# A transformer kernel with a built-in planner: layernorm without its product column, epsilon on GpSimd, DMA transposes planned at new prices

## The chip, the cores and the metric

The kernel runs on one core of one Trainium2 chip. The core has a matrix engine (TensorE, PE in the profile; its weight loads are listed as PEld), three engines for elementwise work (VectorE or DVE, ScalarE or ACT, GpSimd or POOL), and a queue that issues transfers (SyncE, SP). SBUF is the on-chip memory, PSUM the accumulators that TensorE writes, in eight banks of 128 x 512 float32. The metric is device time of one execution in microseconds (us); the median of several runs counts, and less is better.

## The reference

Two layers of a transformer block on 2048 tokens of width 512 in bfloat16, with 32 heads of 16 columns and a hidden width of 1792. Layernorm has no gain and no offset. Both layers use the same weights.

```python
def _layernorm(x, axis=-1, eps=1e-5):
    m = jnp.mean(x, axis=axis, keepdims=True)
    v = jnp.var(x, axis=axis, keepdims=True)
    return (x - m) / jnp.sqrt(v + eps)

def _A_ref(x, wqkv, wo):           # H = 32, Dh = 16
    q, k, v = ...(x @ wqkv)...
    scores = jnp.einsum("bhqd,bhkd->bhqk", q, k) * (Dh ** -0.5)
    o = jnp.einsum("bhqk,bhkd->bhqd", _softmax(scores, axis=-1), v)
    return ...o... @ wo

def _B_ref(x, w1, b1, w2, b2):
    h = _gelu(jnp.einsum("bsd,df->bsf", x, w1) + b1)
    return jnp.einsum("bsf,fd->bsd", h, w2) + b2

x = A_x
x = x + _A_ref(_layernorm(x), A_wqkv, A_wo)
x = x + _B_ref(_layernorm(x), B_w1, B_b1, B_w2, B_b2)
x = x + _A_ref(_layernorm(x), A_wqkv, A_wo)
x = x + _B_ref(_layernorm(x), B_w1, B_b1, B_w2, B_b2)
```

## The kernel before

**Tiles and stages.** The 2048 tokens are 16 tiles of 128 (the partitions) and four chunks of 512. Attention works on cells: a cell is one head, one tile of keys and 512 queries (for the last chunk two heads and 256), 4096 cells in all. A score matmul (L1244) writes a cell into one PSUM bank. Most cells are then exponentiated by ScalarE (L1601), two or three cells to an instruction, into a ring of buffers (`pt`, with parts of `kt`, `q` and `v` lent to it when they are free). The other cells go to VectorE and GpSimd, which approximate the exponential with 16-bit integers: L1396 evicts the cell from PSUM on VectorE, L1473 adds a shift, mostly on GpSimd, and L1478 adds a second shift on VectorE; the buffers are `du`. Only the key tiles listed in `KD` may go that way. A value matmul (L1665) sums either kind of cell into one bank; for a cell of VectorE it takes four of them, three with scaled copies of the values (`vc`). Beside attention, the work of the previous chunk runs: the output projection, the feed-forward part (`hpair`, L976, `gelu`, L997, `ytile`), and the next layer's projections.

**Layernorm** (`ln` and `ln_tile`) comes in groups of one, two or four tiles. For each tile VectorE takes statistics (L666) and aggregates them to a mean and a variance in `mv` (L668). For the group, VectorE adds epsilon (L671, `varr`), GpSimd raises the result to the power -0.5 (L673, `rstd`), and VectorE forms the product -mean x rstd (L676, `nmr`). For each tile one instruction then gives x * rstd + nmr in bfloat16 (L689, `xln`): on GpSimd as a rule, on VectorE where `quick` is set, which holds for the first four tiles of the kernel and the last two. After the GpSimd form a DMA transpose is issued on SP (L693) and lands in `kt`, `xf` or `xp`; after the VectorE form TensorE transposes (L700). The ring `xln` has two buffers, so the third tile's L689 needs the first transpose to have landed.

**The order** of every engine's instructions is fixed when the kernel is built, by a planner written in the kernel (`_Sched`). Threads in Python yield operations (`_Op`) with an engine, a cost, the keys they read and write, and a `tail`, the time from the end of its cost to the landing of a transfer. The planner keeps a clock for each engine, computes when an operation's inputs are ready, and at each step starts the operation that can start first, by priority. `LATENCY` is added between an operation's end and those that wait for it, `OVERLAP` is taken off each VectorE cost, `OWN` and `HEAD` adjust waits on VectorE and on the port that it shares with GpSimd in the planner's model (`port`). `TOL` decides in `attach` whether a free bank may take a VectorE cell, `PSHIFT` in `dchain` whether L1473 goes to GpSimd or to VectorE, `SLACK` and `LATE` how long a score matmul may wait. `fill` puts matmuls without use (L1232, into banks that are free) ahead of a gap of TensorE while the planned activity of the last `WINDOW` microseconds lies below `WARM`. The chosen order is then emitted with semaphore waits; on the chip each engine's queue is strictly in that order, whatever the durations turn out to be. SP's queue holds the loads of weights into an eight-part ring (L933), those of x, the transposes and the stores of the output, also in the planned order.

Of the kernel before, what the change touches and what calls it, by code (L numbers as in the profile page):

```python
# [5 lines left out]
ALU = mybir.AluOpType  # L6
ACT = mybir.ActivationFunctionType
BF16 = mybir.dt.bfloat16
F32 = mybir.dt.float32
# [19 lines left out]
XT = 8  # L29
# [19 lines left out]
OPENING = 18  # L49
ROUNDS = 2  # L50
PTLOW = 5
TOL = 0.2
EVAC = 0.4
MID = 1.4
ENDS = 0.9
QUEUE = 4
RUSH = 4
WINDOW = 3.4
WARM = 2.3
FMARGIN = -0.1  # L60
FOLD = 0.1
COLD = 8
# [8 lines left out]
DWIDE = 2  # L71
RWIDE = 2
AHEAD = 24
PSHIFT = 3
LOG2E = 1.4426950408889634
E_SCALE = 0.25 * LOG2E * 128
E_BIAS = 15992.765054484162
# [6 lines left out]
class _Prog:  # L84
# [4 lines left out]
    def __init__(self, sems):  # L89
        self.sems = sems  # L90
        self.cnt = {k: 0 for k in sems}
        self.prog = {e: [] for e in self.ENGS}
        self.K = {e: {} for e in self.ENGS}
        self.ev_k = {}
        self.lastw = {}
        self.reads = {}
# [89 lines left out]
class _Op:  # L186
    __slots__ = ("eng", "cost", "fns", "reads", "writes", "sem", "by", "tail", "prio", "mode", "slack", "late", "back", "port", "limit", "after")

    def __init__(self, eng, cost, fns, reads=(), writes=(), sem=None, by=1, tail=0.0, prio=None, mode="F", slack=None):
        self.eng, self.cost = eng, cost  # L190
        self.fns = fns if isinstance(fns, list) else [fns]
        self.reads, self.writes = list(reads), list(writes)
        self.sem, self.by, self.tail, self.prio, self.mode, self.slack = sem, by, tail, prio, mode, slack
        self.limit = 1e9
        self.late, self.after = None, []
        self.port = eng == "dve" and self.writes[:1] != [] and self.writes[0].startswith(("OTT", "NMR"))


class _Thread:
# [7 lines left out]
        self.done = False  # L207


OWN = 0.022  # L210
HEAD = 0.14
LATENCY = {"pe": 0.2175, "act": 0.21, "dve": 0.139, "pool": 0.153328, "sp": 0.1}
OVERLAP = 0.083
ROUND = 1.02


class _Sched:
# [76 lines left out]
    def _ready(self, op):  # L294
# [4 lines left out]
        for ev in self.P.deps(op.reads, op.writes):  # L299
            if op.eng == "pe" and ev[0] == "pe":  # L300
                continue
            t = max(t, self.end.get(ev, 0.0) - OWN * (op.eng == "dve" == ev[0]))
        if op.eng == "pe" and op.mode != self.mode:
            t -= SW
        if op.eng == "pool":
            at = max(t, self.clock["pool"])
            for a, b in self.port_ops[-4:]:
                if a <= at < b - HEAD:
                    at = t = b - HEAD
        if op.port and op.eng == "dve":  # L310
            at = max(t, self.clock["dve"])
            for a, b in self.pool_ops[-6:]:
                if a < at + HEAD and at < b - HEAD:
                    at = t = b - HEAD
        return t
# [7 lines left out]
    def _cost(self, op):  # L323
        if op.eng == "act" and op.writes[0][0] in "XKQ":
            return 0.48
        if op.eng == "dve":
            return max(op.cost - OVERLAP, 0.07)
        if op.eng == "pe":
# [11 lines left out]
    def fill(self, start, nxt):  # L340
        while self.filler and self.mode:
# [7 lines left out]
            cold = MM * (now < COLD)  # L349
            if start - now < into + MM + cold + back + FMARGIN or self.active(start) >= WARM:  # L350
                return
# [7 lines left out]
            self.clock["pe"] = now + into + MM + cold  # L359
            self.end[ev] = self.clock["pe"] + LATENCY["pe"]  # L360

    def run(self):
        while True:
# [55 lines left out]
            self.clock[e] = start + cost  # L419
            self.end[ev] = start + cost + op.tail + LATENCY[e]  # L420
            for x in op.after:
# [4 lines left out]
                self.clock[e] = at + MM  # L426
                self.end[ev] = at + MM + LATENCY[e]
            if e == "dve" and op.port:
# [10 lines left out]
def bass_interleave_layers__mha_block__dense_activation_gelu__prompt_kernel(  # L439
# [13 lines left out]
    NT = S // 128  # L453

    with ExitStack() as es:
        def sb(shape, dt, name):
            return es.enter_context(nc.sbuf_tensor(name, shape, dt))

        T = {}
# [41 lines left out]
        T["MV"] = sb([128, NT, 2], F32, "mv")  # L501
        T["VARR"] = sb([128, NT], F32, "varr")
        T["RSTD"] = sb([128, NT], F32, "rstd")
        T["NMR"] = sb([128, NT], F32, "nmr")
        PS = es.enter_context(nc.psum_tensor("ps", [128, 8 * 512], F32))

        sem_names = ["pe", "act", "dve", "pool", "dxt0", "dxt1", "dxt2", "dxt3", "dx1", "dx2", "dx3", "dwq", "dwk", "dwv", "db1", "db2"] + ["dw%d" % c for c in range(3)] + [
# [31 lines left out]
TR = 0.10  # L539
DV = 0.69  # L540
FQ = 2
SLACK = 0.3
LATE = 0.7


class _Plan:
# [112 lines left out]
    def ln(self, tiles, dst, dkeys, prio, quick=False, gate=None):  # L659

        T = self.T
        c, n = tiles[0], len(tiles)
        sl = slice(c, c + n)
        for t in tiles:
            yield ("need", ("xready", t, self.phase[t // 4]))
            yield _Op("dve", 0.66, lambda e, t=t: e.bn_stats(T["STATS"][:, t, :], T["X"][:, t % XT, :]),  # L666
                      reads=["X.%d" % (t % XT)], writes=["ST.%d" % t])
            yield _Op("dve", 0.17, lambda e, t=t: e.bn_aggr(T["MV"][:, t, :], T["STATS"][:, t, :]),  # L668
                      reads=["ST.%d" % t], writes=["MV.%d" % t])
        mvk = ["MV.%d" % t for t in tiles]  # L670
        yield _Op("dve", 0.16, lambda e: e.tensor_scalar(T["VARR"][:, sl], T["MV"][:, sl, 1], 1e-5, None, op0=ALU.add),  # L671
                  reads=mvk, writes=["VARR.%d" % c])
        yield _Op("pool", 0.37 + 0.18 * n, lambda e: e.tensor_tensor(  # L673
            out=T["RSTD"][:, sl], in0=T["VARR"][:, sl], in1=T["NHALF"][:, 0:n], op=ALU.pow),
            reads=["VARR.%d" % c, "NHALF"], writes=["RSTD.%d" % c])
        yield _Op("dve", 0.157, lambda e: e.scalar_tensor_tensor(  # L676
            out=T["NMR"][:, sl], in0=T["MV"][:, sl, 0], scalar=-1.0, in1=T["RSTD"][:, sl], op0=ALU.mult, op1=ALU.mult),
            reads=mvk + ["RSTD.%d" % c], writes=["NMR.%d" % c])
        if gate:
            yield ("need", gate)  # L680
        for t in tiles:
            yield ("spawn", self.ln_tile(c, t, dst, dkeys, quick), prio)

    def ln_tile(self, c, t, dst, dkeys, quick):
        T = self.T
        ph = self.phase[t // 4]
        x = yield ("acq", "xln")
        eng, cost = ("dve", 0.4) if quick else ("pool", 0.77)
        yield _Op(eng, cost, lambda e: e.tensor_scalar(  # L689
            T["XLN"][:, x, :], T["X"][:, t % XT, :], T["RSTD"][:, t:t + 1], T["NMR"][:, t:t + 1], op0=ALU.mult, op1=ALU.add),  # L690
            reads=["X.%d" % (t % XT), "RSTD.%d" % c, "NMR.%d" % c], writes=["XLN.%d" % x])
        if not quick:
            yield _Op("sp", 0.3, lambda e: e.dma_start(dst(t), T["XLN"][:, x, :], transpose=True),  # L693
                      reads=["XLN.%d" % x], writes=dkeys(t), sem="dtr%d" % x, by=16, tail=3.5)
            yield ("rel", "xln", x)
            yield ("give", ("lnt", t, ph))
            return
        b = yield ("acq", "misc")
        tb = self.bank(b).bitcast(BF16)
        fns = [lambda e, dc=dc: e.transpose(tb[:, dc * 128:(dc + 1) * 128], T["XLN"][:, x, dc * 128:(dc + 1) * 128],  # L700
                                            T["IDENT"][:, :]) for dc in range(NDC)]
        yield _Op("pe", 4 * TR, fns, reads=["XLN.%d" % x, "IDENT"], writes=["B.%d" % b], prio=0.8)
        yield ("rel", "xln", x)
        t3 = tb[:, 0:512].rearrange("p (c q) -> p c q", c=NDC)
        if ph == 0 or t % 2 == 0:
            yield _Op("act", DV, lambda e: e.copy(dst(t), t3), reads=["B.%d" % b], writes=dkeys(t))
        else:
            yield _Op("dve", DV, lambda e: e.tensor_copy(dst(t), t3), reads=["B.%d" % b], writes=dkeys(t))
        yield ("rel", "misc", b)
        yield ("give", ("lnt", t, ph))  # L710
# [420 lines left out]
    def route(self, name, b):  # L1131
# [3 lines left out]
        if self.lend == 2:  # L1135
            return "misc"
        return "misc" if q > (0 if b == MISC[0] else QUEUE if self.scored < self.rush else RUSH) or b == MISC[0] else "dbank"

# [186 lines left out]
    def attach(self, op, start, cells, extra, free):  # L1325
# [4 lines left out]
        for home in ("dbank", "misc"):  # L1330
            for b in list(pools[home]):
                if len(used) == 4 or self.lend == 2 or not (self.open or pools["du"]):
                    return
                if any(self.s.end.get(ev, 0.0) > start + TOL for ev in self.P.deps([], ["B.%d" % b]) if ev[0] != "pe"):
                    continue
# [10 lines left out]
    def scores(self):  # L1346
        u = 0
        pools = self.s.pools
        while True:
# [20 lines left out]
            ahead = 0.065 + 0.4267 * self.held[1 - sl]  # L1370
            op = _Op("pe", MM, fns, reads=reads, writes=writes, mode="S", slack=max(SLACK, ahead - LATE))
            op.late = lambda op, start, sl=sl, cells=cells, extra=extra, free=free: (self.attach(op, start, cells, extra, free), self.swap(op, start, cells, extra, free, sl))
# [86 lines left out]
    def dchain(self, pair):  # L1459
# [10 lines left out]
        key = [["DU.%d.%d.%d" % (du, i, j) for j in range(n)] for i in range(4)]  # L1470
        if self.s.clock["pool"] <= self.s.clock["dve"] + PSHIFT and len(pair["cells"]) == n:
            a, b = U[:, 0, 0:n, :].rearrange("p j q -> p (j q)"), U[:, 1, 0:n, :].rearrange("p j q -> p (j q)")
# [300 lines left out]
```

## Time and profile before

| | us |
|---|---|
| three runs | 1523.39, 1520.87, 1520.80 |
| their median | 1520.87 |
| the profiled execution: its span (the page gives no other time for it) | 1522.5 |
| ScalarE busy, idle | 1477.5, 45.0 |
| TensorE busy | 1449.7 |
| VectorE busy | 1333.5 |
| GpSimd busy | 823.6 |
| fillers of TensorE (L1232), all forms | 107 |
| VectorE's evictions of cells (L1396), 955 + 90 | 635.6 + 61.6 |

The profile comes from one execution. A page gives busy time by engine, the span in 40 slices with the clock that TensorE was granted, the chain of work that ended last, and the groups of instructions. A group's row has its line, engine, operation, output and inputs, shapes and count; behind the first bar the busy time and the mean of one in ns; behind the second the idle time of the engine just ahead of these instructions and what ended most of it. L671 is line 671 of the kernel before. Matmuls are pipelined, so a busy TensorE need not be at its peak. A DMA issue on SP is shown as an instruction on SPq.

### The profile page before, as it was taken

Reading aid. Unit: us, or ns where it says so; the run is one execution under the profiler, and the core shown is the slowest. Engines: PE = TensorE matmul, PEld = TensorE weight load, DVE = VectorE, ACT = ScalarE, POOL = GpSimd, SP = SyncE. Lnnn points to the kernel's source line nnn. Section 1 sums busy time; section 2 is a strip of 40 time slices with the busy share of each in tenths; the row PEclk is TensorE's granted clock in tenths of the full one; section 3 lists DMA queues with packets and bytes.
Section 4 is the critical chain, followed back from the end, with each engine's and each line's share of the span. In section 5 each row is a group of like instructions: output and inputs, shape, how many; then the busy total and the mean of one; then the engine's idle time right before and its main releaser. Section 6 shows DMA issues by size and latency. Waiting matters only on the chain.

```text
span 1522.5 us, 46554 instructions
## 1 busy us (share of the span) xinstructions
PE 1449.7 (95%) x20337; PEld 446.0 (29%) x20337; DVE 1333.5 (88%) x2255; ACT 1477.5 (97%) x1374; POOL 823.6 (54%) x783
## 2 busy tenths in 40 slices
PE   8998889999999999999999999899999999999998
PEld 2222222222222222222222222222222222344445
DVE  6568888989999899889989889899989999999994
ACT  7999999999999999999999999999999999999995
POOL 5425545556465554646565466556556656564550
PEclk9999999999999999999999999999999999999999
DMA  5200001144121531125221351001143115412522
GB/s 150 47 2 2 2 2 43 29 126 119 29 57 37 153 92 42 37 62 165 62 57 29 91 141 56 15 2 36 43 139 99 36 29 151 124 37 69 157 68 78
DMA packets 145046, 103.40 MB, mean 68 GB/s; under 512 B 37069, under 2 KB 143822, under 8 KB 144846
## 3 DMA queue, kind: packets, MB, share of 16 engines
q1 hardware_dynamic: 144846, 100.44, 23.4%
q8 instruction: 162, 2.65, 0.7%
q14 instruction: 38, 0.31, 0.1%
HBM read 88.61 MB, written 4.19 MB: 61 GB/s over the span
## 4 chain that ended last, share of the span: by engine, by line
ACT 58%; PE 29%; DVE 10%; issue 1%; POOL 1%; DMA 0%; ACTq 0%; DVEq 0%
ACT pt L1601 47%; PE ps L556 10%; PE ps L1244 9%; PE ps L1665 9%; ACT kt L1601 4%; DVE du L1396 4%; ACT g L997 3%; ACT v L1601 2%; DVE du L1478 2%; ACT q L1601 1%; DVE kt L1396 1%; PE ps L1232 1%; DVE g L976 1%; ACT L1601 1%; ACT L997 1%
## 5 line engine op out<-in xcount | busy, mean ns | idle before, releaser
L1601 ACT ACTIVATE pt<-ps 128x1024 bf16<-128x1024 f32 (+1 forms) x1115 | 1195.5, 1213 | 13.5 <-PE ps L1244 9.2
L1473 POOL TENSOR_SCALAR du<-du 128x1024 uint16<-128x1024 uint16 x478 | 558.6, 1170 | 482.9 <-DVE du L1396 469.3
L1396 DVE TENSOR_SCALAR du<-ps 128x512 uint16<-128x512 f32 x955 | 635.6, 683 | 82.5 <-PE ps L1244 77.6
L1244 PE MATMUL ps<-qp,kt 32*128 32x512 bf16 x4096 | 532.0, 385 | 29.9 <-ACT pt L1601 18.1
L1665 PE MATMUL ps<-pt,v 128*17 128x512 bf16 (+1 forms) x2866 | 400.6, 361 | 11.5 <-ACT pt L1601 7.9
L1665 PE MATMUL ps<-du,vc 128*17 128x512 bf16 (+1 forms) x3213 | 372.9, 359 | 5.0 <-DVE du L1478 2.0
L1478 DVE TENSOR_SCALAR du<-du 128x2048 uint16<-128x2048 uint16 x478 | 350.5, 744 | 12.0 <-POOL du L1473 11.7
L1244 PEld LDWEIGHTS ps<-qp,kt 32*128 32x128 bf16 x4096 | 137.7, 91 | 570.0 <-ACT pt L1601 191.9
L1665 PE MATMUL ps<-du,v 128*17 128x512 bf16 (+1 forms) x1071 | 178.9, 360 | 8.0 <-ACT pt L1601 2.2
L1673 PE MATMUL ps<-vc,zero 128*17 128x512 bf16 x805 | 167.0, 381 | 0.0
L556 PE MATMUL ps<-xf,wr 128*32 128x512 bf16 (+1 forms) x1888 | 129.9, 366 | 2.6 <-DMA xf<-xln 1.3
L1665 PEld LDWEIGHTS ps<-pt,v 128*17 128x17 bf16 x2866 | 98.8, 88 | 108.7 <-issue 64.8
L1665 PEld LDWEIGHTS ps<-du,vc 128*17 128x17 bf16 x3213 | 102.3, 89 | 87.7 <-issue 46.0
L556 PE MATMUL ps<-wr,g 128*32 128x512 bf16 x1600 | 117.4, 382 | 1.9 <-DVE du L1396 1.4
L1192 POOL TENSOR_SCALAR qp<-q,mask 128x512 bf16<-128x512 bf16 (+1 forms) x91 | 76.1, 837 | 63.6 <-PE ps L1244 56.5
L1601 ACT ACTIVATE kt<-ps 128x1536 bf16<-128x1536 f32 (+1 forms) x81 | 102.0, 1268 | 5.0 <-PE ps L1244 3.6
L1473 POOL TENSOR_SCALAR kt<-kt 128x1024 uint16<-128x1024 uint16 x45 | 54.6, 1214 | 75.8 <-DVE kt L1396 74.2
L1601 ACT ACTIVATE v<-ps 128x1024 bf16<-128x1024 f32 (+1 forms) x74 | 85.6, 1187 | 2.7 <-PE ps L1244 1.1
L976 DVE TENSOR_SCALAR g<-ps,hb1t 128x512 bf16<-128x512 f32 (+1 forms) x112 | 79.1, 706 | 7.3 <-PE ps L556 7.2
L1396 DVE TENSOR_SCALAR kt<-ps 128x512 uint16<-128x512 f32 x90 | 61.6, 684 | 14.0 <-PE ps L1244 12.3
L1665 PE MATMUL ps<-kt,v 128*17 128x512 bf16 (+1 forms) x314 | 71.1, 365 | 1.4 <-DVE kt L818 0.6
L1665 PEld LDWEIGHTS ps<-du,v 128*17 128x17 bf16 x1071 | 45.8, 89 | 55.0 <-issue 25.6
(90 smaller groups left out, 1242.9 us busy)
## 6 DMA issues: line engine op xcount, KB each, us to landing
wr<-in_B_w_dram SPq DMA_DIRECT2D x256, 256.0 KB, 2.9
wr<-in_A_wqkv_dram SPq DMA_DIRECT2D x24, 256.0 KB, 3.0
wr<-in_A_wo_dram SPq DMA_DIRECT2D x18, 256.0 KB, 2.9
x<-in_A_x_dram SPq DMA_DIRECT2D x7, 512.0 KB, 4.5
kept<-x SPq DMA_DIRECT2D x4, 512.0 KB, 2.9
x<-kept SPq DMA_DIRECT2D x4, 512.0 KB, 3.9
out_dram<-x SPq DMA_DIRECT2D x16, 128.0 KB, 2.8
g<-in_A_wqkv_dram SPq DMA_DIRECT2D x3, 512.0 KB, 5.9
```

Source lines behind the costliest of these rows:

```text
L556: return [lambda e, a=a: e.matmul(out[32 * a:32 * a + 32, :], lhsT=lhsT[:, 32 * a:32 * a + 32], rhs=rhs, start=start, stop=stop, tile_posi ...
L976: yield _Op("dve", 0.21 + n / 966, lambda e, fc=fc, pb=pb: e.tensor_scalar(T["G"][:, fc, q], pb, T["HB1T"][:, fc:fc + 1], None, op0=ALU.ad ...
L997: lambda e, g=g: e.activation(out=g, in_=g, func=ACT.Gelu_apprx_tanh), reads=gk, writes=gk, prio=2)
L1192: yield _Op("pool", 0.27 + 0.42 * w / 512, lambda e, s=s, q=q, i=i, t=t, w=w: e.tensor_scalar(T["QP"][:, s, w * i:w * i + w], q, T["MASK"] ...
L1232: fns.append(lambda e, o=o, w=w, a=a, m=m: e.matmul(o, lhsT=w, rhs=rhs, start=start, stop=start, tile_position=(0, m * a)))
L1244: return (lambda e: e.matmul(o, lhsT=lhsT, rhs=rhs, start=True, stop=True, tile_position=(32 * a, 0)), ["K%d.%d.%d" % (l, gb, kt // 4), "Q ...
L1396: yield _Op("dve", 0.682, lambda e: e.tensor_scalar(u, self.bank(b), E_SCALE, E_BIAS, op0=ALU.mult, op1=ALU.add), reads=["B.%d" % b], writ ...
L1473: one = _Op("pool", 0.15 + 0.45 * n, lambda e, a=a, b=b: e.tensor_scalar(b, a, float(SHIFT), 1.0, op0=ALU.add, op1=ALU.mult), reads=key[0] ...
L1478: two = _Op("dve", 0.152 + 0.266 * n, lambda e: e.tensor_scalar(U[:, 2:4, 0:n, :], U[:, 0:2, 0:n, :], 2 * SHIFT, None, op0=ALU.add), reads ...
L1601: yield _Op("act", 0.065 + 0.4267 * n, lambda e, src=src, dst=dst: e.activation(out=dst, in_=src, func=ACT.Exp, scale=0.25), reads=["B.%d" ...
L1665: op.fns.append(lambda e, o=o, lhsT=q[0][0][m], rhs=q[0][1][:, n * m:n * m + n], a=a, st=st, sp=sp: e.matmul(o, lhsT=lhsT, rhs=rhs, start= ...
L1673: op.fns.append(lambda e, o=self.bank(b)[32 * a:32 * a + 17, :], rhs=rhs, a=a, st=not begun[a], sp=end: e.matmul(o, lhsT=T["ZERO"][:, 0:17 ...
```

## The change

Four things change. The product `nmr` and its operation are gone: `ln_tile` subtracts the mean, read from `mv`, and multiplies by `rstd` in one instruction with the same shape. The addition of epsilon moves from VectorE to GpSimd, written as an addition and a multiplication by 1.0. The planner prices the DMA transpose at 1.25 on SP's queue and 3.2 to landing, where it had 0.3 and 3.5. And nine constants of the planner (thirteen numbers, since `LATENCY` holds five) get other values. These and the prices bear on the order only.

```diff
-TOL = 0.2
+TOL = 0.209826292977
...
+TTAIL = 3.2
...
-WARM = 2.3
+WARM = 2.217891545089
...
-PSHIFT = 3
+PSHIFT = 2.847157765011
...
-        self.port = eng == "dve" and self.writes[:1] != [] and self.writes[0].startswith(("OTT", "NMR"))
+        self.port = eng == "dve" and self.writes[:1] != [] and self.writes[0].startswith("OTT")
...
-OWN = 0.022
-HEAD = 0.14
-LATENCY = {"pe": 0.2175, "act": 0.21, "dve": 0.139, "pool": 0.153328, "sp": 0.1}
-OVERLAP = 0.083
+OWN = 0.021958568758
+HEAD = 0.133062372179
+LATENCY = {"pe": 0.210086274943, "act": 0.212153888496, "dve": 0.142808970582, "pool": 0.154691936953, "sp": 0.097779777626}
+OVERLAP = 0.085489581326
...
-SLACK = 0.3
-LATE = 0.7
+SLACK = 0.298025012106
+LATE = 0.682703432516
...
-        yield _Op("dve", 0.16, lambda e: e.tensor_scalar(T["VARR"][:, sl], T["MV"][:, sl, 1], 1e-5, None, op0=ALU.add),
+        yield _Op("pool", 0.15, lambda e: e.tensor_scalar(T["VARR"][:, sl], T["MV"][:, sl, 1], 1e-5, 1.0, op0=ALU.add, op1=ALU.mult),
                   reads=mvk, writes=["VARR.%d" % c])
...
-        yield _Op("dve", 0.157, lambda e: e.scalar_tensor_tensor(
-            out=T["NMR"][:, sl], in0=T["MV"][:, sl, 0], scalar=-1.0, in1=T["RSTD"][:, sl], op0=ALU.mult, op1=ALU.mult),
-            reads=mvk + ["RSTD.%d" % c], writes=["NMR.%d" % c])
...
-            T["XLN"][:, x, :], T["X"][:, t % XT, :], T["RSTD"][:, t:t + 1], T["NMR"][:, t:t + 1], op0=ALU.mult, op1=ALU.add),
-            reads=["X.%d" % (t % XT), "RSTD.%d" % c, "NMR.%d" % c], writes=["XLN.%d" % x])
+            T["XLN"][:, x, :], T["X"][:, t % XT, :], T["MV"][:, t, 0:1], T["RSTD"][:, t:t + 1], op0=ALU.subtract, op1=ALU.mult),
+            reads=["X.%d" % (t % XT), "MV.%d" % t, "RSTD.%d" % c], writes=["XLN.%d" % x])
...
-            yield _Op("sp", 0.3, lambda e: e.dma_start(dst(t), T["XLN"][:, x, :], transpose=True),
-                      reads=["XLN.%d" % x], writes=dkeys(t), sem="dtr%d" % x, by=16, tail=3.5)
+            yield _Op("sp", 1.25, lambda e: e.dma_start(dst(t), T["XLN"][:, x, :], transpose=True),
+                      reads=["XLN.%d" % x], writes=dkeys(t), sem="dtr%d" % x, by=16, tail=TTAIL)
```

More of the change, by code (lines that the diff above doesn't have):

```diff
@@ L503, in bass_interleave_layers__mha_block__dense_activation_gelu__prompt_kernel @@
         T["RSTD"] = sb([128, NT], F32, "rstd")
-        T["NMR"] = sb([128, NT], F32, "nmr")
         PS = es.enter_context(nc.psum_tensor("ps", [128, 8 * 512], F32))
```

## The prediction

> **What bounds the kernel now.** I read the page first: busy shares, the clock row, the chain. Then the waits, the windows of 180 us and of 2 us, the groups of the layernorm lines, and the timelines of the opening, of 224 to 252 us and of the last 30 us. From the page, busy us of each engine:
> ```profile
> PE 1449.7 (95%) x20337; PEld 446.0 (29%) x20337; DVE 1333.5 (88%) x2255; ACT 1477.5 (97%) x1374; POOL 823.6 (54%) x783
> ```
> ScalarE leaves 45.0 us of the 1522.5 us span idle. Windows of 20 us place them: 8.1 in the first 20 us, 15.4 after 1500, and 21.6 in all between. What the change can win in the middle is at most those 21.6 us plus exponentials that move from ScalarE to VectorE. The windows of 180 us (columns: length, then busy us and count on PE, PEld, DVE, ACT, POOL, then clock, DMA share, GB/s) show how even it is:
> ```profile
> 240.00:420.00 180.00, 173.51 (x2256) 47.93 (x2256) 161.76 (x269) 175.25 (x168) 102.37 (x90) 0.98 0.24 69
> 420.00:600.00 180.00, 174.48 (x2317) 49.28 (x2313) 171.22 (x290) 177.31 (x171) 102.89 (x95) 1.00 0.27 76
> ```
> ScalarE idles 4.8 and 2.7 us there. The first of the two holds the worst spot of the run; in windows of 2 us:
> ```profile
> 246.00:248.00 2.00, 0.65 (x11) 0.27 (x12) 1.39 (x3) 1.44 (x2) 1.42 (x1) 0.88 0.00 0
> 248.00:250.00 2.00, 2.00 (x19) 0.24 (x11) 0.56 (x1) 0.56 (x1) 0.00 (x0) 0.50 0.00 0
> 250.00:252.00 2.00, 2.00 (x18) 0.33 (x14) 1.48 (x3) 1.49 (x2) 1.04 (x1) 0.50 0.00 0
> 252.00:254.00 2.00, 2.00 (x18) 0.34 (x19) 1.32 (x3) 1.05 (x2) 0.77 (x1) 0.50 0.00 0
> ```
> TensorE runs dry at 246, its granted clock falls to 0.50 for some 7 us, and ScalarE loses 3.5 us between 240 and 260 (16.48 busy of 20). The chain of waits names the cause: the last transpose of a layernorm, on the path with everything ahead of it.
> ```profile
> 235.75 1.51 POOL xln L689 x2
> 237.27 1.01 POOL du L1473
> 238.28 0.59 POOL ott L844
> 238.87 1.45 POOL du L1473
> 240.32 2.46 POOL xln L689 x2
> 242.77 0.51 POOL du L1473
> 243.28 4.39 DMA xf<-xln
> ```
> One more dip, at 213 to 218, has no layernorm near it and costs 1.1 us of ScalarE. Elsewhere the clock reads 1.00.
>
> **The change, part by part.** The sum is made against the profiled execution, span 1522.5 us; the page gives nothing else around it. It lies 1.6 us above the median of the runs, 1520.87, and inside their range, so a difference from the span is applied to the median.
>
> *VectorE loses two small operations per group of tiles.* There are 25 groups (columns: count, then busy us and mean ns, then idle before):
> ```profile
> L673 POOL TENSOR_TENSOR rstd<-varr,nhalf 128x4 f32<-128x4 f32 (+2 forms) x25 | 24.3, 981 | 26.0 <-DVE varr L671 25.3
> L671 DVE TENSOR_SCALAR varr<-mv 128x4 f32<-128x4 f32 (+2 forms) x25 | 6.4, 260 | 0.3
> L676 DVE SCALAR_TENSOR_TENSOR nmr<-mv,rstd 128x4 f32<-128x4 f32 (+2 forms) x25 | 4.8, 196 | 2.3 <-POOL rstd L673 2.0
> ```
> That is 6.4 + 4.8 = 11.2 us of VectorE. A cell of scores taken by VectorE costs it 683 ns (L1396) and half of 744 ns (L1478), 1.06 us; it saves ScalarE about 0.42 us, the difference of a three-cell and a two-cell exponential in the chain (1.34 and 0.92). All 11.2 us turned into cells: 10.6 cells, 4.5 us off ScalarE. None turned: nothing. VectorE still has 8.8 us idle in its fullest window above, so its time is not the only limit on cells; I take half, -2.2.
>
> *GpSimd gains 25 epsilon additions.* The trace has no such small TENSOR_SCALAR on POOL. Bounds: the memset of 128x4, 0.10 us, and the power of one column, 0.58. Nearest in kind is L1192, 602 ns at 256 columns and 887 at 512, which extrapolates to 0.32 at none; I take that, 25 x 0.32 = 8 us on an engine 54% busy. Ahead of the power, POOL now idles 25.3 us waiting for the VectorE addition, so outside the opening this is covered. If that cover goes, the evictions of POOL queued behind (L1473) come late, and then L1478 on VectorE, which waits 11.7 us for POOL already. On GpSimd the result passes to the power through GpSimd's own semaphore; such a step cost 0.24 us at the start (L566 behind L565).
>
> *Mean and rstd as two scalars.* L689 keeps its engine, shape and two per-partition operands, so 0 on 768 ns; same form, same bounds. It no longer waits for L676 (5.4 us of POOL idle in 10 waits, longest 0.8). At 235 us the product ended at 235.64, 1.05 us after the power, since VectorE did two evictions first.
>
> *The planner's price of a DMA transpose.* Before: 0.3 on the queue, 3.5 to landing, 0.1 latency: 3.9. After: 1.25 + 3.2 + 0.1 = 4.55. The trace says 1.23 median on SP and 4.39 from start to landing:
> ```profile
> L693 SPq DMA_TRANSPOSE xf<-xln x30: 1188/1226/2222, 236.5 to 1461.7; - x30
> ```
> And of the waits of PE, in us, times and the longest, the only one for a transpose:
> ```profile
> PE ps L556 <- DMA xf<-xln: 1.3, 1, 1.3
> ```
> It is the place above. Four transposes fill SP from 236.54 to 244.54. With 0.95 more for each on the queue, the plan asks for the first matmul of the feed-forward part 1 to 4 us later and puts score and value work ahead of it. The stall and its clock dip cost 3.5 us; the next thing late there are POOL's transposed normals themselves (2.46 us for two instead of 1.54), so I take -2.5, bounds -3.5 and 0. Weight loads queue behind these transposes on SP, but no wait of PE names a weight load, so that stays hidden. What stood late in POOL behind L689 (6.0 us waiting for a landing, 5.4 for L676) feeds the 11.7 us that VectorE waits for POOL: 11.7 / 1.06 x 0.42 = 4.6 at most, nothing at least; I take a third, -1.5.
>
> *Opening.* POOL runs a memset until about 5.0, then four powers to 7.39; the last normalisation starts at 7.77. Four additions, 1.28, enter that row; gone are 0.23 of idle and 0.26 of the product's share behind the last power: +0.8 (0.10 each: -0.1; 0.58 each: +1.8).
>
> *End.* Two additions move to POOL (+0.64, against 0.27 on VectorE); the normalisation there already waits behind L1029 until 1503.82, and 0.22 of products go: -0.15 (bounds -0.3 and +0.4).
>
> *The other constants* (overlap, latencies, thresholds, the fill threshold 2.3 to 2.218) reprice nothing on the chip but redraw the order of all that follows. The overlap is nearer to the rows: pairs of L1396 in the chain take 1.19, 0.595 each; the plan had 0.599 and gets 0.597. The size of a redraw: ScalarE's idle time in the six full 180 us windows is 4.8, 2.7, 2.4, 0.3, 3.6 and 2.6 us, standard deviation 1.5; two draws over 8.5 such windows differ by 1.5 x 1.41 x 2.9 = 6 us. I take 0 for it, with 6 either way. That is larger than any single term and is most of the range.
>
> Sum: -2.2 - 2.5 - 1.5 + 0.8 - 0.15 = -5.6, so span 1516.9, median 1515.3.
>
> **A rule beside the clock rows.** Fewer fillers could bring more dips. In the trace a gap of 1.35 us, after thin work, was enough for half clock. The Trainium skill, "TensorE: Matmul & The Clock Gate", section "What's actually happening", gives half rate after at least one idle window of about 3.4 us. By that rule alone no idle time in this trace would trip the gate, fewer fillers would cost nothing and the slower rival below would fall away; the two dips of the trace came with no idle time above 1.35 us, so I go by the trace.
>
> **The rivals.**
> *Slower: the clock.* The fill threshold falls 3.6%, so the planner stops filling sooner. Fillers carry most in 60 to 240 us (26.1 us of PE) and 960 to 1040 (16.2), where real work is thin. For it: both dips follow thin stretches (PE 1.13 and 0.65 busy of 2 us). Against: in both an actual wait (0.85 and 1.35 us) came first. A dip costs 1.1 to 3.5 us of ScalarE. From three at the high price on it decides (5.6 + 3.0 is 8.6); four: 14 us, 1515.3 + 14 = 1529. Chance 0.17.
> *Slower: GpSimd late.* Epsilon at the high bound, 0.58, and its semaphore, 0.24, in POOL's queue: 0.82 for each of the 19 groups behind the opening and ahead of the end, 15.6 us that reach L1478; at 0.42 for 1.06 that is +6.2. The layernorm at 235 us then gains nothing and its stall stays (+2.5), and the opening goes to its high bound (+1.0): -5.6 + 9.7 = +4.1, 1525. It decides from two thirds of the 15.6 us on. For it: L1478's 11.7 us of waits. Against: POOL idles 482.9 us ahead of L1473. Chance 0.09.
> *Hidden anyway.* The stall at 247 moves to another group and freed VectorE time stays idle: 1521. For it: PE waits for a transpose in one group of nineteen only. Chance 0.12.
> *Better.* All of the relief (-4.5), stall and dip gone (-3.5, -1.1), late POOL work gone (-4.6), opening as taken: -13, 1508. For it, VectorE above 95% of several 20 us windows. Against, it needs every term. Chance 0.14.
>
> **How the numbers follow.** The forecast has 0.48, with its own range 1511 to 1519. About 0.2%, 3 us, is what a measurement can tell from no change. Faster is below 1517.8: 0.45 of the forecast's 0.48 and the 0.14 of the better case, 0.59. Within 3 us: 0.03 and the hidden case, 0.15. Slower: 0.17 + 0.09 = 0.26. The range reaches from the better case, less 3 us of redraw, 1505, to the clock case, 1529; a tenth lies outside on each side.
>
> **What would show it.** Right: L671 on POOL 25 times near 0.3 us, L676 absent; no wait of PE for a transpose near 240 and no clock below 0.9 there; more than 1045 evictions of L1396 and fewer ScalarE cells than 3051; ScalarE idle in the middle below 18 us. Wrong: new dips in the clock row, above all at 60 to 240 and 960 to 1040; a POOL wait that grows ahead of L1478; or as many cells on VectorE as now, with its 11 us idle.

## The result, and the profile after

The changed kernel takes 1569.26 us in the median of its runs, against 1520.84 us of the kernel before in the same comparison: a ratio of 1.0316, 95% interval 1.0302 to 1.0331. The forecast was 1515.3, between 1505 and 1529. The profiled execution has a span of 1568.2 us, 45.7 more than the one before. Engines and clock, from part 1 of the page of the changed kernel:

```profile
PE 1452.9 (93%) x20054; PEld 438.5 (28%) x20054; DVE 1333.1 (85%) x2203; ACT 1482.8 (95%) x1376; POOL 906.9 (58%) x807
```

ScalarE's busy time grew by 5.3 us and its idle time by 40.4, to 85.4. The engine that did more is GpSimd, +83.3 us. The groups of the layernorm (columns as before: count, busy us and mean ns, idle us ahead) say on what, first the normalisation of the kernel before, then the changed kernel:

```profile
L689 POOL TENSOR_SCALAR xln<-x,rstd,nmr 128x512 bf16<-128x512 bf16 x58 | 53.3, 923 | 12.1 <-DVE nmr L676 5.4 <-DMA kt<-xln 4.7 <-DMA xf<-xln 1.3
L689 DVE TENSOR_SCALAR xln<-x,rstd,nmr 128x512 bf16<-128x512 bf16 x6 | 2.4, 411 | 0.1
...
L686 POOL TENSOR_SCALAR xln<-x,mv,rstd 128x512 bf16<-128x512 bf16 x58 | 132.4, 2286 | 2.3 <-DMA kt<-xln 0.7
L673 POOL TENSOR_TENSOR rstd<-varr,nhalf 128x4 f32<-128x4 f32 (+2 forms) x25 | 23.3, 934 | 1.7
L671 POOL TENSOR_SCALAR varr<-mv 128x4 f32<-128x4 f32 (+2 forms) x25 | 8.7, 349 | 28.3 <-DVE mv L668 26.9
L686 DVE TENSOR_SCALAR xln<-x,mv,rstd 128x512 bf16<-128x512 bf16 x6 | 2.5, 412 | 2.7 <-POOL rstd L673 2.7
```

The normalisation on GpSimd, same shape and again two per-partition operands, went from 923 to 2286 ns, 53.3 to 132.4 us in all. On VectorE it kept its time, 411 and 412 ns. Epsilon on GpSimd is small, 349 ns each in the mean, as forecast. The first feed-forward layernorm shows what follows, in the chain of waits of the changed kernel (start us, us, what):

```profile
244.21 1.04 POOL rstd L673
245.25 0.09 issue
245.33 1.05 POOL du L1470
246.38 1.03 POOL ott L841
247.40 5.07 POOL xln L686 x2
252.48 1.03 POOL du L1470
253.50 0.02 issue
253.53 0.69 DVE du L1475
254.22 0.61 DVE du L1393
254.83 0.05 issue
254.88 0.60 PE ps L1241
255.48 1.82 PE ps L1229 x12
```

Two normalisations hold GpSimd for 5.07 us (the four of before took 1.51 and 2.46 for two at a time). Behind them stands an ordinary shift of attention cells, L1470; VectorE's L1475 waits for it, the next eviction stands behind L1475 on VectorE, and the score matmul waits for the bank. So the layernorm stops attention, not only the layernorm's own consumers. In windows of 2 us (length, then busy us and count on PE, PEld, DVE, ACT, POOL, then clock, DMA share, GB/s):

```profile
250.00:252.00 2.00, 1.59 (x28) 0.39 (x20) 1.07 (x2) 2.00 (x3) 2.00 (x2) 1.00 0.18 38
252.00:254.00 2.00, 1.02 (x11) 0.20 (x8) 0.47 (x1) 2.00 (x2) 2.00 (x3) 0.99 0.33 67
254.00:256.00 2.00, 1.12 (x9) 0.37 (x13) 1.30 (x3) 1.88 (x2) 2.00 (x1) 0.50 0.28 35
256.00:258.00 2.00, 2.00 (x24) 0.41 (x12) 0.21 (x1) 0.00 (x0) 2.00 (x3) 0.50 0.32 65
258.00:260.00 2.00, 2.00 (x19) 0.38 (x15) 1.36 (x2) 1.45 (x1) 2.00 (x2) 0.50 0.01 0
```

GpSimd is full throughout. TensorE thins out, its clock falls to 0.50, and ScalarE stands for two whole microseconds. Counting stretches of 2 us windows with a clock below 0.95 after the first 60 us, there are eight ahead of the end, at 254, 382, 454, 638, 826, 926, 1222 and 1390 us, where the kernel before had two (212 and 246). GpSimd normalises at or within 4 us ahead of each. At two of the eight (454 and 826) TensorE stood waiting for a transpose, 3.22 and 1.78 us; at the other six it waited for a shift (L1470) that stood behind a normalisation, or for VectorE's instructions behind that shift. The eight 20 us windows that hold most of these dips (from 240, 380, 440, 640, 820, 920, 1220 and 1380 on) lack 29.8 us of ScalarE. The waits of the whole run (total us, times, longest) say it once more:

```profile
ACT pt L1598 <- PE ps L1241: 40.9, 47, 3.8
DVE du L1475 <- POOL du L1470: 35.9, 32, 3.9
PE ps L556 <- DMA xf<-xln: 5.0, 2, 3.2
```

Before, the third was 1.3 us in one wait, and the first two were:

```profile
ACT pt L1601 <- PE ps L1244: 9.2, 18, 1.1
DVE du L1478 <- POOL du L1473: 11.7, 20, 1.6
```

Of the 40.4 us that ScalarE idles more, 33.8 lie in the middle (54.4 us idle from 60 to 1540 us, against 20.6 from 60 to 1500 before). Another 6.4 are in the first 60 us: the first exponential starts at 15.57 us instead of 12.77, and from 20 to 60 us ScalarE is busy 35.3 instead of 39.0. The stretch behind the last exponential is the same, 26.6 and 26.5 us.

### The profile page after: what moved, and what is told of

Same layout as the page of the kernel before. It is cut to its first block, busy times and chain, and to the rows that moved or that the text cites. A ratio compares the mean times of both kernels' runs of the same rounds, so it can differ in the third digit from the quotient of the medians.

```text
span 1568.2 us, 45982 instructions
## 1 busy us (share of the span) xinstructions
PE 1452.9 (93%) x20054; PEld 438.5 (28%) x20054; DVE 1333.1 (85%) x2203; ACT 1482.8 (95%) x1376; POOL 906.9 (58%) x807
## 4 chain that ended last, share of the span: by engine, by line
PE 37%; ACT 35%; DVE 15%; POOL 11%; issue 1%; DMA 1%; SPq 0%; POOLq 0%; DVEq 0%; ACTq 0%
ACT pt L1598 28%; PE ps L556 13%; PE ps L1241 12%; PE ps L1662 11%; POOL xln L686 6%; DVE du L1393 6%; DVE du L1475 3%; POOL du L1470 3%; ACT g L994 2%; ACT kt L1598 2%; DVE stats L666 1%; POOL rstd L673 1%; ACT v L1598 1%; DVE g L973 1%; DVE x L878 1%
## 5 line engine op out<-in xcount | busy, mean ns | idle before, releaser
L1470 POOL TENSOR_SCALAR du<-du 128x1024 uint16<-128x1024 uint16 x477 | 559.7, 1175 | 499.1 <-DVE du L1393 483.4
L1241 PE MATMUL ps<-qp,kt 32*128 32x512 bf16 x4096 | 537.9, 388 | 55.0 <-ACT pt L1598 28.9
L1475 DVE TENSOR_SCALAR du<-du 128x2048 uint16<-128x2048 uint16 x477 | 355.4, 757 | 36.2 <-POOL du L1470 35.9
L1662 PE MATMUL ps<-du,v 128*17 128x512 bf16 (+1 forms) x1072 | 173.6, 361 | 13.4 <-POOL du L1470 4.8
L1670 PE MATMUL ps<-vc,zero 128*17 128x512 bf16 x768 | 160.6, 383 | 0.0
L686 POOL TENSOR_SCALAR xln<-x,mv,rstd 128x512 bf16<-128x512 bf16 x58 | 132.4, 2286 | 2.3 <-DMA kt<-xln 0.7
L1598 ACT ACTIVATE kt<-ps 128x1536 bf16<-128x1536 f32 (+1 forms) x89 | 111.6, 1270 | 8.5 <-PE ps L1241 7.0
L1598 ACT ACTIVATE v<-ps 128x1024 bf16<-128x1024 f32 (+1 forms) x81 | 94.7, 1216 | 3.4 <-PE ps L1662 1.3
L1662 PE MATMUL ps<-kt,v 128*17 128x512 bf16 (+1 forms) x334 | 79.7, 373 | 1.6 <-ACT pt L1598 1.2
L1470 POOL TENSOR_SCALAR kt<-kt 128x1024 uint16<-128x1024 uint16 x45 | 50.3, 1117 | 44.6 <-DVE kt L1393 44.4
```

The lines of the kernel that those rows point to most:

```text
L686: yield _Op(eng, cost, lambda e: e.tensor_scalar(T["XLN"][:, x, :], T["X"][:, t % XT, :], T["MV"][:, t, 0:1], T["RSTD"][:, t:t + 1], op0=A ...
L1241: return (lambda e: e.matmul(o, lhsT=lhsT, rhs=rhs, start=True, stop=True, tile_position=(32 * a, 0)), ["K%d.%d.%d" % (l, gb, kt // 4), "Q ...
L1470: one = _Op("pool", 0.15 + 0.45 * n, lambda e, a=a, b=b: e.tensor_scalar(b, a, float(SHIFT), 1.0, op0=ALU.add, op1=ALU.mult), reads=key[0] ...
L1475: two = _Op("dve", 0.152 + 0.266 * n, lambda e: e.tensor_scalar(U[:, 2:4, 0:n, :], U[:, 0:2, 0:n, :], 2 * SHIFT, None, op0=ALU.add), reads ...
L1598: yield _Op("act", 0.065 + 0.4267 * n, lambda e, src=src, dst=dst: e.activation(out=dst, in_=src, func=ACT.Exp, scale=0.25), reads=["B.%d" ...
L1662: op.fns.append(lambda e, o=o, lhsT=q[0][0][m], rhs=q[0][1][:, n * m:n * m + n], a=a, st=st, sp=sp: e.matmul(o, lhsT=lhsT, rhs=rhs, start= ...
```

## The experiments

**Which property of the instruction is slow.** Ten forms alone on GpSimd, in a kernel that computes nothing of the reference.

```diff
+                lambda: e.tensor_scalar(y, x, o, t, op0=ALU.mult, op1=ALU.add),
+                lambda: e.tensor_scalar(y, x, p, o, op0=ALU.subtract, op1=ALU.mult),
+                lambda: e.tensor_scalar(y, x, t, o, op0=ALU.subtract, op1=ALU.mult),
+                lambda: e.tensor_scalar(y, x, t, o, op0=ALU.add, op1=ALU.mult),
+                lambda: e.tensor_scalar(y, x, o, t, op0=ALU.mult, op1=ALU.subtract),
+                lambda: e.tensor_scalar(y, x, p, o, op0=ALU.mult, op1=ALU.add),
+                lambda: e.tensor_scalar(y, x, o, 1.0, op0=ALU.mult, op1=ALU.mult),
+                lambda: e.tensor_scalar(y, x, t, 1.0, op0=ALU.subtract, op1=ALU.mult),
+                lambda: e.tensor_scalar(y, x, 0.5, 2.0, op0=ALU.subtract, op1=ALU.mult),
+                lambda: e.tensor_scalar(TWO[:, 4:8], PAIR[:, 4:8, 1], 1e-5, 1.0, op0=ALU.add, op1=ALU.mult),
```

Expected:

> This kernel computes nothing of the reference: it copies x to the output and runs ten forms of the tensor_scalar instruction on GpSimd, six times each, one after the other with nothing beside them, on 128x512 bfloat16 (the last on 128x4 float32). In order: multiply then add with two per-partition scalars (the form of before); subtract then multiply with the mean read at a step of two, as in the changed kernel; the same with both scalars in plain columns; add then multiply; multiply then subtract; multiply then add with the first scalar at a step of two; multiply by a scalar then by 1.0; subtract a scalar then multiply by 1.0; subtract 0.5 then multiply by 2.0; and the addition of epsilon. Theory A (the operation pair is slow on GpSimd): the first takes 0.76 us, the second and third 2.07, and the sixth 0.76. Theory B (the scalar read at a step of two is slow): the second and the sixth take 2.07, the third 0.76. Theory C (the form is not slow by itself, VectorE's work beside it is): all at 0.76. For the epsilon addition 0.20 in each theory.

Measured, in groups by form (L31 is the first line of the diff, L40 the last):

```profile
L35 POOL TENSOR_SCALAR y<-x,one,two 128x512 bf16<-128x512 bf16 x6 | 12.4, 2074 | 0.6
L32 POOL TENSOR_SCALAR y<-x,pair,one 128x512 bf16<-128x512 bf16 x6 | 12.4, 2073 | 0.6
L33 POOL TENSOR_SCALAR y<-x,two,one 128x512 bf16<-128x512 bf16 x6 | 12.4, 2072 | 0.6
L38 POOL TENSOR_SCALAR y<-x,two 128x512 bf16<-128x512 bf16 x6 | 12.0, 1998 | 0.6
L39 POOL TENSOR_SCALAR y<-x 128x512 bf16<-128x512 bf16 x6 | 11.5, 1922 | 0.5
...
L34 POOL TENSOR_SCALAR y<-x,two,one 128x512 bf16<-128x512 bf16 x6 | 4.6, 769 | 0.6
L36 POOL TENSOR_SCALAR y<-x,pair,one 128x512 bf16<-128x512 bf16 x6 | 4.6, 768 | 0.6
L31 POOL TENSOR_SCALAR y<-x,one,two 128x512 bf16<-128x512 bf16 x6 | 4.6, 767 | 1.9 <-DMA x<-in_A_x_dram 1.4
L37 POOL TENSOR_SCALAR y<-x,one 128x512 bf16<-128x512 bf16 x6 | 4.1, 690 | 0.6
L40 POOL TENSOR_SCALAR two<-pair 128x4 f32<-128x4 f32 x6 | 1.2, 194 | 0.5
```

Theory A holds: every form with a subtraction takes 1.92 to 2.07 us, first or second, with scalars or with constants; every form of additions and multiplications takes 0.69 to 0.77. The step of two in the scalar's column costs nothing (L36), and the slow forms are slow with no work of VectorE beside them.

**The old form in the changed kernel.**

```diff
+        yield _Op("dve", 0.157, lambda e: e.scalar_tensor_tensor(
+            out=T["NMR"][:, sl], in0=T["MV"][:, sl, 0], scalar=-1.0, in1=T["RSTD"][:, sl], op0=ALU.mult, op1=ALU.mult), ...
-            ..., T["MV"][:, t, 0:1], T["RSTD"][:, t:t + 1], op0=ALU.subtract, op1=ALU.mult),
+            ..., T["RSTD"][:, t:t + 1], T["NMR"][:, t:t + 1], op0=ALU.mult, op1=ALU.add),
```

> The changed kernel with the product nmr on VectorE and multiply-then-add restored; epsilon on GpSimd, the prices and the constants stay as changed. Theory (the slow normalisation on GpSimd made all of the loss): GpSimd's normalisation is back near 0.9 us, and the time within 10 us of before, 1511 to 1531. Rival (prices and constants made the loss): 1555 to 1570.

1531.37 us, ratio 1.0069 (1.0052 to 1.0086). The normalisation is at 767 ns in the median (count, then minimum, median and maximum ns, then the first and the last start in us):

```profile
L690 POOL TENSOR_SCALAR xln<-x,rstd,nmr x58: 754/767/2311, 24.4 to 1475.6; 128x512 bf16<-128x512 bf16 x58
```

37.9 of the 48.4 us are gone. It misses the expected bound of 1531 by little, and it leaves 10.5 us that the normalisation does not explain.

**The new form in the kernel before.**

```diff
-        yield _Op("dve", 0.157, lambda e: e.scalar_tensor_tensor(out=T["NMR"]...
-            ..., T["RSTD"][:, t:t + 1], T["NMR"][:, t:t + 1], op0=ALU.mult, op1=ALU.add),
+            ..., T["MV"][:, t, 0:1], T["RSTD"][:, t:t + 1], op0=ALU.subtract, op1=ALU.mult),
```

> The kernel before with only the new normalisation: subtract the mean, multiply by rstd, no product nmr. Prices, constants and the place of epsilon as before. Theory (slow normalisation): normalisation near 2.3 us, time 1555 to 1575, with clock dips behind the groups of four transposes. Rival (prices and constants): 1515 to 1525.

1586.89 us, ratio 1.0433 (1.0410 to 1.0455): 66 us more than before, above the expected range, and worse than the whole change. The normalisation takes 2237 ns in the mean, and TensorE waits for transposes in eight places, where there was one:

```profile
L685 POOL TENSOR_SCALAR xln<-x,mv,rstd 128x512 bf16<-128x512 bf16 x58 | 129.6, 2237 | 3.4 <-DMA kt<-xln 1.4 <-DMA xf<-xln 0.6
...
PE ps L555 <- DMA xf<-xln: 11.6, 5, 4.4
PE ps L555 <- DMA xp<-xln: 2.4, 2, 1.6
PE ps L555 <- DMA kt<-xln: 2.4, 1, 2.4
```

In the changed kernel, where the transpose has its higher price, this is 5.0 us in two places. That fits a higher price that softened the blow of the slow form; the two kernels differ in the constants too, so it isn't shown.

**The planner told of the slow form.**

```diff
-        eng, cost = ("dve", 0.4) if quick else ("pool", 0.77)
+        eng, cost = ("dve", 0.4) if quick else ("pool", 2.08)
```

> The changed kernel, with one number in it changed: the planner prices the normalisation on GpSimd at 2.08 where it has 0.77. Nothing else is different on the chip but the order. Theory that the loss is one of the order (the plan is wrong about when normals land, TensorE waits, the clock dips): most of the loss goes, 1520 to 1540. Rival that the loss is GpSimd's 79 us more of work, which takes its time wherever it stands: 1555 to 1570, as changed.

1549.23 us, ratio 1.0186 (1.0171 to 1.0202), between the two expectations. The normalisation still takes 2193 ns in the mean, but no wait of TensorE for a transpose is left, VectorE's wait of L1475 for GpSimd is back at 13.6 us, and the mean clock is 0.998 (0.983 in the changed kernel). A right price takes 20 of the 38 us away. The other 18, against the old form in the same kernel, stay: GpSimd is 59 us busier than with the old form, and how much of the 18 is that and how much another draw of the order was not separated.

**Time on GpSimd without a subtraction.** The kernel before, with a power over six constant columns behind each normalisation.

```diff
+        more = lambda e: e.tensor_tensor(out=T["DUO"][:, :], in0=T["DUI"][:, :], in1=T["DUI"][:, :], op=ALU.pow)
+        yield _Op(eng, cost, [real] if quick else [real, more], ...
```

> The kernel before with its own normalisation (multiply, then add), and behind each of the 58 on GpSimd a power over six columns of a constant into a scratch tile, 1.3 us of GpSimd that nobody reads; the transpose waits for both, and the planner's cost is unchanged. Theory (time in GpSimd's queue ahead of the transpose is all that matters): 1560 to 1590, like the new form in the kernel before (1587), with clock dips behind the layernorms. Rival (the subtracting form hurts in another way, such as the port that GpSimd shares with VectorE): 1525 to 1545, and few dips.

1593.3 us, ratio 1.0490 (1.0463 to 1.0516), just above the expected range, and about where the subtraction puts this kernel (1586.89). The added operation took 1393 ns:

```profile
L694 POOL TENSOR_TENSOR duo<-dui 128x6 f32<-128x6 f32 x58 | 80.8, 1393 | 0.0
```

There are thirteen dips of the clock after the first 60 us, and L1484 (the kernel's L1478) waits 50.7 us for GpSimd. So the same time in GpSimd's queue hurts as much without a subtraction; that the subtracting form harms in some other way is not needed to explain the loss.

**The rest of the change, one part at a time**, each in the kernel before: epsilon on GpSimd; the transpose's price; the nine constants.

```diff
-        yield _Op("dve", 0.16, lambda e: e.tensor_scalar(T["VARR"][:, sl], T["MV"][:, sl, 1], 1e-5, None, op0=ALU.add),
+        yield _Op("pool", 0.15, lambda e: e.tensor_scalar(T["VARR"][:, sl], T["MV"][:, sl, 1], 1e-5, 1.0, op0=ALU.add, op1=ALU.mult),
```

> The kernel before with epsilon added on GpSimd and nothing else changed. Theory that the 10.5 us that the changed kernel keeps with the old form restored are one redraw of the order: 1514 to 1530, either side of before. Rival that epsilon on GpSimd costs them: 1527 to 1535, with more waits of VectorE's L1478 for GpSimd than the 11.7 us of before.

1528.51 us, ratio 1.0052 (1.0036 to 1.0069). The time lies in both expected ranges and does not decide between them. L1478 waits 13.6 us for GpSimd, hardly more than 11.7, so the rival's reason is not seen in the middle. A cost in the opening is: the first exponential starts at 15.65 instead of 12.77 us. Four additions stand between the powers in GpSimd's row behind its memset, VectorE's four normalisations start from 6.28 to 9.31 us instead of from 5.88 to 7.77, and the 32 matmuls of the first projection take longer (start us, us, what; the kernel before, then this one):

```profile
9.54 1.91 PE L556 MATMUL ps<-kt,g 128*32 128x512 bf16 x32 [0.77 <-ACT kt L706]
11.15 3.11 PE L556 MATMUL ps<-kt,g 128*32 128x512 bf16 x32 [0.22 <-ACT kt L706]
```

The clock column reads 1.00 there in both, so the trace does not say why they are slow. The late start belongs to epsilon and not to a draw of the order: the first exponential starts between 15.31 and 16.11 us in all five kernels here that have epsilon on GpSimd, and between 12.39 and 13.19 in the eight others that run the two layers. It is 2.9 of the 8 us here, of which ScalarE's busy time lacks 2.2 by 60 us; where the rest comes from was not traced.

```diff
-            yield _Op("sp", 0.3, lambda e: e.dma_start(dst(t), T["XLN"][:, x, :], transpose=True), ... tail=3.5)
+            yield _Op("sp", 1.25, lambda e: e.dma_start(dst(t), T["XLN"][:, x, :], transpose=True), ... tail=3.2)
```

> The kernel before with the planner's price of a DMA transpose at 1.25 and 3.2 instead of 0.3 and 3.5, nothing else. By the prediction's step the stall at 247 us goes: 1515 to 1520, no wait of TensorE for a transpose. Theory of a redraw: 1514 to 1530 whatever happens at that stall. Rival that the price costs the 10.5 us: 1527 to 1535.

1518.22 us, ratio 0.9986 (0.9977 to 0.9995). The spot that the prediction began with is whole; the window of 20 us (columns as in the windows above), in this kernel:

```profile
240.00:260.00 20.00, 19.47 (x252) 5.26 (x248) 19.31 (x30) 19.88 (x20) 14.67 (x13) 1.00 0.19 41
```

and in the kernel before:

```profile
240.00:260.00 20.00, 18.13 (x198) 4.34 (x202) 14.96 (x24) 16.48 (x17) 11.73 (x10) 0.83 0.11 27
```

ScalarE gains 3.4 us there, and 0.9 from 200 to 220 us, where the other dip is gone too; the whole kernel gains 2.3, so some was lost elsewhere. It is the fastest kernel of this study, by less than the 0.2% that the prediction takes for no change.

```diff
-WARM = 2.3
+WARM = 2.217891545089
... (and TOL, PSHIFT, OWN, HEAD, LATENCY, OVERLAP, SLACK, LATE as changed)
```

> The kernel before with the nine changed constants of the planner (TOL, WARM, PSHIFT, OWN, HEAD, LATENCY, OVERLAP, SLACK, LATE), nothing else. Theory of a redraw: 1514 to 1530. Rival that these constants cost the 10.5 us: 1527 to 1535. Rival of the prediction, that the lower fill threshold brings clock dips: 1525 to 1535 with three or more dips in thin stretches.

1529.02 us, ratio 1.0060 (1.0045 to 1.0075), inside all three expected ranges. Fillers fell from 26.05 to 21.72 us between 60 and 240 us, and from 16.22 to 12.11 between 960 and 1040, and the clock stayed at 1.00 in both stretches. There is one dip in the middle, at 674. In the changed kernel, too, fillers fell there, to 21.10 and 8.74 us, at a clock of 1.00 and without a dip. The rival of the fill threshold falls.

**What a redraw of the order is worth.** Two changes of a planner's constant by an amount that means nothing.

```diff
-HEAD = 0.14
+HEAD = 0.141
```

> The kernel before with HEAD at 0.141 instead of 0.140, one nanosecond in the planner, which means nothing on the chip but gives another order of most instructions. Theory (a redraw by itself moves the time by several us, the sum's term of 0 with 6 either way): 1513 to 1530 and clear of 1520.5 by 2 us or more. Rival (redraws are small, so epsilon and constants cost 8 us each by what they do): within 2 us of 1520.5.

1524.1 us, ratio 1.0025 (1.0016 to 1.0035).

```diff
-OVERLAP = 0.083
+OVERLAP = 0.0831
```

> The kernel before with OVERLAP at 0.0831 instead of 0.083, a tenth of a nanosecond for each VectorE operation in the planner; again only the order differs. Theory of large redraws: 1513 to 1530 and clear of 1520.5 by 2 us or more. Rival of small redraws: within 2 us of 1520.5.

1528.94 us, ratio 1.0053 (1.0038 to 1.0068). A tenth of a nanosecond in the plan costs 8.3 us, as much as the nine constants or epsilon on GpSimd. Both redraws also left VectorE fewer cells: 942 + 88 and 945 + 88, against 955 + 90.

**Two versions without a subtraction.** In the changed kernel (its edit is shown), and in the kernel before with the transpose's price, where VectorE forms the negated mean:

```diff
+        yield _Op("pool", 0.15, lambda e: e.tensor_scalar(T["NMR"][:, sl], T["MV"][:, sl, 0], -1.0, 1.0, op0=ALU.mult, op1=ALU.mult), ...
-            ..., T["MV"][:, t, 0:1], T["RSTD"][:, t:t + 1], op0=ALU.subtract, op1=ALU.mult),
+            ..., T["NMR"][:, t:t + 1], T["RSTD"][:, t:t + 1], op0=ALU.add, op1=ALU.mult),
```

> The changed kernel with its normalisation as (x + negated mean) * rstd, add then multiply; the negated mean is one more small operation on GpSimd behind epsilon. Theory (the subtraction alone is slow): normalisation at 0.77 us in the median, time near the old form's 1531: 1522 to 1536. Rival (applying mean and rstd as two scalars is slow as such): 1560 or more.

> A version meant to keep what was sound: the kernel before with the transpose priced at 1.25 and 3.2, (x + negated mean) * rstd, the negated mean on VectorE right behind epsilon, both ahead of the power; epsilon and the constants as before. Theory: VectorE's product is off the chain between the power and the normals, the stall at 247 us is gone, 1511 to 1520; a redraw can take 6 us either way. Rival (only the redraw counts): 1520 to 1530.

1534.62 us, ratio 1.0093 (1.0077 to 1.0110), and 1532.63 us, ratio 1.0076 (1.0061 to 1.0091). The first is as expected:

```profile
L689 POOL TENSOR_SCALAR xln<-x,nmr,rstd x58: 754/767/1708, 23.0 to 1469.3; 128x512 bf16<-128x512 bf16 x58
```

Mean and rstd as two scalars are fast if the mean is added. The second lies above both of its expected ranges, nearer to the rival's. What the shorter chain bought, if anything, and what the new order took can't be told apart; VectorE took 942 + 90 cells, 13 fewer than before.

## Why the prediction was wrong

**The step that failed** is "L689 keeps its engine, shape and two per-partition operands, so 0 on 768 ns; same form, same bounds". Engine, shape and operands were the same, the arithmetic operation was not, and on GpSimd that is worth 1.3 us for each of 58 tiles. The form alone, undone, takes 37.9 of the 48.4 us away, and put alone into the kernel before it adds 66. The prediction bounded the epsilon addition, for which the trace had no row, from 0.10 to 0.58 and gave the normalisation, for which it had no row either (none subtracts on GpSimd), the bounds of a row with another operation. A wider bound on the same step would have opened the range upward. The rows at hand gave a reason for one: a power costs GpSimd some 0.15 us per column (0.56 us for one, 1.03 for four at the start of the kernel before), while a normalisation of 512 columns takes 0.77, so the operation matters there far more than the shape.

The Trainium skill, "GPSIMD Engine Reference", section "Engine selection", calls one-input elementwise work on GpSimd roughly line rate and only two-input work about twice as slow as VectorE. The runs don't bear out the first part: with multiplication and addition the normalisation takes 768 ns there against 411 on VectorE, 1.9 times, and with a subtraction 2.07 us against 0.41, five times. The measurements decide.

**Point by point.**

- *VectorE's relief, -2.2.* Wrong: 0. With epsilon on GpSimd and the old form, VectorE's busy time falls from 1333.5 to 1327.3 us, about the 6.4 that moved, and ScalarE keeps its 3051 cells; the changed kernel leaves it one more (954 + 90 evictions of VectorE). No kernel here has more than the 1045 evictions of before, so time freed on VectorE did not become cells in any of them; what does limit its cells was not tested.
- *Epsilon, 0.32 us on POOL.* The operation takes 0.19 to 0.20 in the median, inside the bounds, with 0.35 in the mean. In the middle it is covered, as said: L1478 waits 13.6 us for GpSimd with epsilon there alone, against 11.7.
- *The transpose's price, -2.5.* Right in the mechanism and the place: the stall at 247 us and its dip are gone. That the whole gives -2.3, so near the term, is luck in part, since a redraw of the order alone moves the time by more.
- *Late work in POOL, -1.5.* Wrong even without the slow form: VectorE waits 14.0 us for GpSimd with the old form in the changed kernel, where it waited 11.7.
- *Opening, +0.8.* The last of its four normalisations does come 0.97 us later (8.74 instead of 7.77), but ScalarE's first exponential comes 2.8 us later. The term counted GpSimd's row and left out that TensorE's first projection runs slower behind it: 32 matmuls in 3.61 us, at a granted clock of 0.50, instead of 1.91.
- *End, -0.15.* +0.1 by the stretch behind the last exponential. The term does not follow from its own figures either: 0.64 - 0.27 - 0.22 is +0.15.
- *The redraw, 0 with 6 either way.* The size was about right and the centre was not. Two redraws that mean nothing gave +3.5 and +8.3 us. With the six kernels that normalise fast and differ from the one before in a part, the eight lie from -2.3 to +14.0 us, 7.8 in the mean (by each median, from the 1520.5 to 1520.9 measured beside it). The order before looks like a good draw, so that any other is more likely to lose; with two pure redraws this is likely and not shown. The spread over its own windows, from which the term was worked out, cannot show it. Of the 10.5 us that the changed kernel keeps with the old form, the late start of the first exponential (16.11 instead of 12.77 us) is 3.3; the rest has the size of a redraw and was not separated.
- *The rivals.* Dips of the clock did come, but from stalls behind GpSimd and not by the fill threshold; how much of the loss is the clock and how much the stalls themselves was not separated. The nearest was "GpSimd late": its place and its chain (POOL, then L1478) are what happened, at 0.82 us for each group instead of 1.36 for each tile, and it was given 0.09. Its threshold of two thirds is too low as well: for the 8.6 us that the clock needs to decide, GpSimd must give 5.1 of its 6.2 beside the other 3.5, five sixths.
- *What would make it wrong* named the right two rows, dips and L1478's wait for POOL, though no dip came in the two stretches that it named.

In the changed kernel the dip at 254 came when TensorE had been busy 1.59 and 1.02 us of the 2 us windows ahead of it, its longest gap being 1.24 us. The Trainium skill, "TensorE: Matmul & The Clock Gate", section "What's actually happening", gives half rate after at least one idle window of about 3.4 us; here, too, the clock fell after a shorter gap in thin work, so the measurement decides.

## What to carry to other kernels

Price an instruction by a row with the same engine and the same arithmetic operation; equal shape and operands are not enough, and where no row has the operation, bound it as unknown. An instruction that grows on a lightly loaded engine can do harm through what is queued behind it: here GpSimd was 54% busy, and 1.3 us more for a normalisation, where a shift of cells stood behind it, held up VectorE, TensorE and then ScalarE. In a kernel whose order comes from a planner, measure what a meaningless change of a constant does, before a difference of half a percent is laid to any cause.

## What the runs showed of the hardware that was not expected

- A tensor_scalar of 128x512 bfloat16 on GpSimd takes 0.69 to 0.77 us with additions and multiplications, and 1.92 to 2.07 with a subtraction in either place. VectorE shows no such difference between multiply-then-add and subtract-then-multiply (411 and 412 ns).
- 1.3 us more on GpSimd for each of 58 tiles, 74 to 81 us in all on an engine with 700 us to spare, cost 38 to 73 us of the run in the three kernels whose planner did not know of it, and some 18 in the one whose planner did; each of these holds a redraw of the order as well.
